# Strips of 64 bytes between the seven left operands of a linear attention block with SwiGLU

## The chip, the core and the metric

The kernel runs on one core of a Trainium2 chip. The core has TensorE (matmuls; PE in the profile, its weight loads PEld), VectorE (DVE), ScalarE (ACT), GpSimd (POOL) and SyncE (SP), a working memory of 128 partitions (SBUF), an accumulator memory of eight banks (PSUM), and DMA engines that move data to and from the main memory. The metric is the device time of one execution in microseconds (us); the median of several runs is given.

## What is computed

For x of 2048 x 1024 (float32):

```python
xn = _layernorm(x, axis=-1)
s = _A_ref(xn, A_wqkv, A_wo)          # linear attention, 32 heads of 32
g = _silu(_B_ref(xn, B_w1, B_w3, B_w2))
return x + s * g
```

`_A_ref` takes q, k and v from one product with `wqkv` (1024 x 3072), applies `phi(t) = where(t > 0, t + 1, exp(t)) + 1e-6` to q and k, forms `kv = phi(k)^T v` and the sum of `phi(k)` for each head, divides `phi(q) kv` by `phi(q)` times that sum, and multiplies with `wo` (1024 x 1024). `_B_ref` is `(silu(xn w1) * (xn w3)) w2` with 3584 hidden columns.

## The kernel before

**Products.** Every large product is cut in two along each of its three dimensions, and the eight products of blocks are replaced by seven, with sums of blocks formed beforehand and afterwards (Strassen's scheme in Winograd's form). The seven right operands are called `B11, T2, T3, T1, B21, T4, B22`, their left partners `A11, S2, S3, S1, A12, A22, S4`. Each operand is held as two parts of a shorter type (`split`, L95 and L96: ScalarE rounds to the high part, VectorE subtracts to get the low part), and each product of tiles is three matmuls (`mm3`, L103 to L105): high by high, high by low, low by high. A wide matmul has a stationary operand of 128 x 128 and a moving operand of 128 x 512.

**Stages.** The tokens are taken in two halves of 1024.

1. For the first half the rows of x are loaded, normalised and turned (transposes by TensorE, L164), which fills the seven left operands, one tile a name: `operand_tiles` makes them, each of 128 partitions x 2 parts x 4 slices x 512 columns, 16,384 bytes in a partition. For the second half they are prepared meanwhile, kept in main memory (`a_d`), and loaded into the same seven places.
2. `gemm` (L447 to L499) forms one block of 256 output columns for all tokens of a half: 7 products of 4 slices x 3 matmuls, 84 matmuls. The stationary operands are the weights' tiles of the pool `pb`; the moving operands are the seven left operands, in the order A11, S2, S3, S1, A12, A22, S4. Each half has 36 such calls: 4 for keys, 4 for queries, 28 for the gate and up projections. In places two calls run side by side, product by product.
3. Between the keys and queries of the second half and its projections, `row_products` forms xn^T phi(k) (tiles `xy`, all in `pb`, into banks `g`).
4. During the second half's projections smaller work is put between the products by `catch_up`: denominators, `key_values`, and `merge_wo` (L943 and around), whose matmuls have the stationary operand `kvm` of the pool `st` and the moving operand `wos` of `pb`.
5. Attention: its right operands (`wp`, from `attention_right`) are put into the seven places of the left operands, four tiles of 4,096 bytes to a place; they are the moving operands here. The stationary ones are `X...` tiles in `pb`.
6. The second layer of the SwiGLU (`layers`): its right operands lie in the pool `pw`, which takes over the memory of the seven places and of what follows; stationary are again `X...` tiles in `pb`.

**Order.** Instructions are recorded in the order that the program writes them out, and a scheduler of the framework orders them by a simulated timeline; `tc.issue_after` pins a few. Each engine then runs its own list in order; semaphores tie them together. Loads go out on SP's queue, most stores on GpSimd's.

**Places in memory.** Pools lie one after another in a partition, in the order in which they are opened: `const`, `pb` (8 x 4,096 bytes), `pe`, `pc`, `pa` (the seven places), `praw`, `st`; `pw` is opened after `pa`, `praw` and `st` are closed. Every tile is rounded up to 32 bytes. The constants contain a tile `gap` of 79 floats (316 bytes, 320 with rounding) that nothing reads or writes. The places that matter, in bytes from the start of a partition, and their remainders modulo 512:

| tile | before | mod 512 | after | mod 512 |
|---|---|---|---|---|
| first of `pb` (stationary operands) | 17,984 | 64 | 17,664 | 256 |
| A11 | 77,376 | 64 | 77,056 | 256 |
| S2 | 93,760 | 64 | 93,504 | 320 |
| S3 | 110,144 | 64 | 109,952 | 384 |
| S1 | 126,528 | 64 | 126,400 | 448 |
| A12 | 142,912 | 64 | 142,848 | 0 |
| A22 | 159,296 | 64 | 159,296 | 64 |
| S4 | 175,680 | 64 | 175,744 | 128 |
| first of `praw` | 192,064 | 64 | 192,256 | 256 |
| `kvm` (in `st`) | 227,968 | 128 | 228,160 | 320 |
| first of `pw` (after `pa` is closed) | 77,376 | 64 | 77,056 | 256 |

The last tile ends at 228,992 bytes before and at 229,184 after, of 229,376.

Of the kernel before, what the change touches and what calls it, by code (L numbers as in the profile page):

```python
# [9 lines left out]
F32 = mybir.dt.float32  # L10
FR = mybir.dt.float32r
# [5 lines left out]
P = 128  # L17
C = 512
# [4 lines left out]
def tile_linear_attention_times_swiglu(  # L23
# [14 lines left out]
    ND = D // P  # L38
# [8 lines left out]
    const = ctx.enter_context(tc.tile_pool(name="const", bufs=1))  # L47
# [12 lines left out]
    for i in range(P // DH):  # L60
        nc.vector.memset(hmask[i * DH:(i + 1) * DH, i * DH:(i + 1) * DH], 1.0)

    const.tile([P, 79], F32, name="gap")
    zacc = const.tile([P, ND], F32, name="zacc")
    nc.vector.memset(zacc, 0.0)

# [16 lines left out]
    AOPS = ["A11", "S2", "S3", "S1", "A12", "A22", "S4"]  # L83
# [28 lines left out]
    pa = era1.enter_context(tc.tile_pool(name="pa", bufs=1))  # L112
# [53 lines left out]
        return turned, low  # L166

    def operand_tiles(h):
        return {n: pa.tile([P, 2, ND // 2, C], FR, tag=n, name=f"{n}_{h}") for n in AOPS}

    def keep_rows(h, i, n, t):

# [474 lines left out]

    def half(h):
        A = operand_tiles(h)

        def keys(pair, **how):
# [494 lines left out]
    def hiddens(i, m):  # L1146
        return left(m, lambda n: h_d[i][m // NT][:, PLACE[n][m % NT]], (FB[i][1] - FB[i][0]) // 2, f"B{i}")
# [7 lines left out]
    def second_weights(i, n, k):  # L1155
        if (i, n, k) not in asked:
            ask(i, n, k, small)
        return asked[i, n, k]
# [110 lines left out]
    def layer_place(n, i, k):  # L1269
# [4 lines left out]
                      lambda n, _, k, i=i: second_weights(i, n, k),  # L1274
                      lambda m, i=i: hiddens(i, m), lambda m, t, n: acc[m][:, t, n],
# [32 lines left out]
```

## Time and profile before

| | |
|---|---|
| median of 3 runs | 2347.4 us (2346.8 to 2353.08) |
| the profiled execution | 2349.84 us, its span 2348.1 us |
| TensorE busy | 2300.6 us (98% of the span), 10,368 matmuls |
| VectorE, ScalarE, GpSimd busy | 76%, 39%, 29% |
| moved by DMA | 479.69 MB, 204 GB/s |

The span runs from the first to the last instruction. A busy share is an average over stages; matmuls overlap one another, so a duration (about 390 ns for a wide one) is longer than the distance from one start to the next. In a row of a timeline the first number is the start in us, the second the duration in us; in a row by line, three numbers with strokes are minimum, median and maximum of the duration in ns. A name before the arrow is what an instruction writes, those after it what it reads; buffer numbers are left out, so `A` stands for A11, A12 and A22, and `S` for S1 to S4.

### The profile page before, as it was taken

Reading aid. Unit: us, or ns where it says so; the run is one execution under the profiler, and the core shown is the slowest. Engines: PE = TensorE matmul, PEld = TensorE weight load, DVE = VectorE, ACT = ScalarE, POOL = GpSimd, SP = SyncE. Lnnn points to the kernel's source line nnn. Section 1 sums busy time; section 2 is a strip of 40 time slices with the busy share of each in tenths; the row PEclk is TensorE's granted clock in tenths of the full one; section 3 lists DMA queues with packets and bytes.
Section 4 is the critical chain, followed back from the end, with each engine's and each line's share of the span. In section 5 each row is a group of like instructions: output and inputs, shape, how many; then the busy total and the mean of one; then the engine's idle time right before and its main releaser. Section 6 shows DMA issues by size and latency. Waiting matters only on the chain.

```text
span 2348.1 us, 30976 instructions
## 1 busy us (share of the span) xinstructions
PE 2300.6 (98%) x10368; PEld 1890.5 (81%) x10368; DVE 1780.3 (76%) x2830; ACT 924.7 (39%) x1639; POOL 689.8 (29%) x854
## 2 busy tenths in 40 slices
PE   6999999999999999999999999999999999999997
PEld 5788888888887888777888888888887888888876
DVE  8887888888777775657867788887745666766798
ACT  5555343433232555433332433334324534242433
POOL 4220333376866221001423344342310000000033
PEclk9999999999999999999999999999999999999999
DMA  6555455576668646776756666665656566665688
GB/s 233 179 184 180 153 184 184 170 226 218 226 209 314 221 146 202 253 258 203 224 180 183 191 193 212 205 213 174 224 158 196 180 188 176 222 215 177 192 267 258
DMA packets 353695, 479.69 MB, mean 204 GB/s; under 512 B 24208, under 2 KB 262800, under 8 KB 353424
## 3 DMA queue, kind: packets, MB, share of 16 engines
q1 hardware_dynamic: 315808, 357.63, 48.2%
q0 software_dynamic: 37728, 120.09, 15.6%
q8 instruction: 81, 1.33, 0.2%
q14 instruction: 78, 0.64, 0.1%
HBM read 306.71 MB, written 174.59 MB: 205 GB/s over the span
## 4 chain that ended last, share of the span: by engine, by line
PE 73%; issue 5%; DVE 4%; DMA 3%; ACT 1%; POOL 0%; SPq 0%; DVEq 0%; POOLq 0%; ACTq 0%
PE g L103 2%; PE g L104 2%; PE g L105 2%; PE dB L104 1%; PE dB L105 1%; PE dB L103 1%; PE aB L103 1%; PE cB L103 1%; PE cB L104 1%; PE aB L104 1%; PE aB L105 1%; PE cB L105 1%; PE bB L105 1%; PE bB L104 1%; PE bB L103 1%
## 5 line engine op out<-in xcount | busy, mean ns | idle before, releaser
L750 POOL DMA_DIRECT2D h_d<-sg x112 | 82.8, 740 | 256.8 <-DVE sg L746 166.3
L1063 POOL DMA_DIRECT2D u_d<-uB x32 | 17.3, 541 | 407.6 <-DVE uB L1046 345.8
L96 DVE TENSOR_TENSOR xy<-xy,xy 128x512 fp32r<-128x512 f32 x112 | 72.9, 686 | 65.4 <-ACT xy L95 65.3
L95 ACT CAST xy<-xy 128x512 fp32r<-128x512 f32 x112 | 65.1, 619 | 102.0 <-PE g L105 58.4
L104 PE MATMUL g<-xy,xy 128*128 128x512 f32 x224 | 87.8, 392 | 0.3 <-DVE xy L96 0.2
L105 PE MATMUL g<-xy,xy 128*128 128x512 f32 x224 | 87.3, 390 | 0.0
L103 PE MATMUL g<-xy,xy 128*128 128x512 f32 x224 | 82.7, 398 | 0.0
L517 POOL DMA_DIRECT2D y_d<-y x48 | 34.6, 721 | 140.0 <-ACT y L537 79.9
L1046 DVE TENSOR_TENSOR acc<-cB,acc 128x512 f32<-128x512 f32 x50 | 34.4, 689 | 42.9 <-PE cB L105 42.9
L1046 DVE TENSOR_TENSOR acc<-dB,acc 128x512 f32<-128x512 f32 x56 | 38.6, 689 | 30.8 <-PE dB L105 30.6
L730 POOL TENSOR_TENSOR hs<-hs,sg 128x256 f32<-128x256 f32 x56 | 60.5, 1081 | 0.1
L732 POOL TENSOR_TENSOR hs<-sg 128x256 f32<-128x256 f32 x56 | 57.3, 1023 | 0.0
L103 PEld LDWEIGHTS g<-xy,xy 128*128 128x128 f32 x224 | 41.8, 188 | 14.2 <-issue 4.5
L888 POOL DMA_DIRECT2D qs_d<-qd x32 | 18.1, 564 | 117.5 <-DVE qd L884 80.1
L1177 POOL DMA_DIRECT2D s_d<-s x32 | 17.3, 541 | 117.4 <-DVE s L1046 69.2
L733 POOL TENSOR_TENSOR hs<-sg,hs 128x256 f32<-128x256 f32 x56 | 50.6, 903 | 1.4
L104 PEld LDWEIGHTS g<-xy,xy 128*128 128x128 f32 x224 | 42.1, 188 | 10.2 <-DVE xy L96 1.4
L729 POOL TENSOR_TENSOR hs<-sg,sg 128x256 f32<-128x256 f32 x56 | 49.7, 887 | 1.2
L765 POOL TENSOR_TENSOR w<-w 128x256 f32<-128x256 f32 x28 | 28.2, 1007 | 73.0 <-DMA w<-in_B_w 73.0
L105 PEld LDWEIGHTS g<-xy,xy 128*128 128x128 f32 x224 | 42.1, 188 | 8.8
L758 POOL DMA_DIRECT2D h_d<-hs x60 | 45.8, 765 | 3.5 <-POOL hs L733 2.4
L95 ACT CAST XS4B<-rS4B 128x384 fp32r<-128x384 f32 (+1 forms) x40 | 19.7, 493 | 60.7 <-PE cB L105 41.1
(5315 smaller groups left out, 8326.9 us busy)
## 6 DMA issues: line engine op xcount, KB each, us to landing
h_d<-hs POOLq DMA_DIRECT2D x60, 256.0 KB, 3.3
h_d<-sg POOLq DMA_DIRECT2D x56, 256.0 KB, 3.7
w<-in_B_w SPq DMA_DIRECT2D x56, 256.0 KB
wt_d<-w SPq DMA_DIRECT2D x28, 512.0 KB
xy<-x_d SPq DMA_DIRECT2D x28, 512.0 KB
xy<-y_d SPq DMA_DIRECT2D x28, 512.0 KB
h_d<-hs SPq DMA_DIRECT2D x52, 256.0 KB
y_d<-y POOLq DMA_DIRECT2D x48, 256.0 KB, 3.1
```

Source lines behind the costliest of these rows:

```text
L95: nc.scalar.copy(out=hi, in_=src)
L96: return nc.vector.tensor_sub(out=lo, in0=src, in1=hi.bitcast(F32))
L103: nc.tensor.matmul(acc, lhsT=wh, rhs=ah, start=start, stop=False, skip_group_check=True)
L104: nc.tensor.matmul(acc, lhsT=wh, rhs=al, start=False, stop=False, skip_group_check=True)
L105: return nc.tensor.matmul(acc, lhsT=wl, rhs=ah, start=False, stop=stop, skip_group_check=True)
L729: e.tensor_add(out=s1, in0=a21, in1=a22)
L730: e.tensor_sub(out=s2, in0=s1, in1=a11)
L732: e.tensor_sub(out=s3, in0=a11, in1=a21)
L733: e.tensor_sub(out=s4, in0=a12, in1=s2)
L750: nc.gpsimd.dma_start(out=h_d[i][2 * h + c][:, 2 * n:4 * n + 2, k], in_=src)
L758: queue.dma_start(out=h_d[i][2 * h + c][:, 6 + 4 * e:10 + 4 * e, k], in_=o[e].rearrange("p (e s) -> p e s", s=P))
L1046: return V.tensor_add(out=c, in0=src, in1=c)
```

## The change

The tile `gap` goes, and `operand_tiles` makes, behind each of the seven left operands, a tile that nothing uses: 16 floats (64 bytes) behind the first six, 32 floats (128 bytes) behind the last. Both halves use the same seven places and strips, and so does attention. `pb`, `pe` and `pc` begin 320 bytes lower, `praw` and `st` 192 bytes higher.

```diff
-    const.tile([P, 79], F32, name="gap")
     zacc = const.tile([P, ND], F32, name="zacc")
     nc.vector.memset(zacc, 0.0)
...
     def operand_tiles(h):
-        return {n: pa.tile([P, 2, ND // 2, C], FR, tag=n, name=f"{n}_{h}") for n in AOPS}
+        A = {}
+        for i, n in enumerate(AOPS):
+            A[n] = pa.tile([P, 2, ND // 2, C], FR, tag=n, name=f"{n}_{h}")
+            pa.tile([P, 16 if i < 6 else 32], F32, tag=f"step{i}", name=f"step{i}_{h}")
+        return A
```

## The prediction, made before the changed kernel was run

> **What bounds the kernel now.** I read the page first: shares of busy time, the clock, the chain that ended last.
>
> ```profile
> span 2348.1 us, 30976 instructions
> PE 2300.6 (98%) x10368; PEld 1890.5 (81%) x10368; DVE 1780.3 (76%) x2830; ACT 924.7 (39%) x1639; POOL 689.8 (29%) x854
> PEclk9999999999999999999999999999999999999999
> PE 73%; issue 5%; DVE 4%; DMA 3%; ACT 1%; POOL 0%; SPq 0%; DVEq 0%; POOLq 0%; ACTq 0%
> ```
>
> TensorE (PE) works through 98% of the span with its clock at 9 tenths or more in every slice, and the chain is TensorE for 73%: what lengthens a matmul lengthens the kernel, nearly one for one. The list of waits shows single events at its head (total, times, longest, in us):
>
> ```profile
> PE tA L164 <- DVE v L148: 11.4, 1, 11.4
> PE bk__735 L103 <- ACT S L95: 4.7, 1, 4.7
> PE cB L103 <- DVE acc L1046: 3.1, 1, 3.1
> ```
>
> Then the pace of the matmuls, from two stretches of the table of windows in which TensorE never stops:
>
> ```profile
> 1400.00:1600.00 200.00, 200.00 (x884) 165.79 (x883) 167.25 (x292) 62.28 (x104) 84.35 (x104) 1.00 0.66 207
> 1900.00:2200.00 300.00, 300.00 (x1325) 248.76 (x1324) 200.24 (x349) 99.59 (x189) 11.35 (x21) 1.00 0.60 185
> ```
>
> After the stretch come its length and TensorE's busy time with its matmuls. 200/884 and 300/1325 give 226.3 ns from start to start, in the gate and up products as in the second layer. The program has 9,792 of these 128x512 matmuls: 72 calls of `gemm` x 7 products x 12 = 6,048; row products 672; attention 672; second layer 2,352; `merge_wo` 48. Times 226.3 ns that is 2,216 of 2,348 us. So the question is whether addresses can move this pace. By line (min/median/max of a duration in ns, first and last start):
>
> ```profile
> L103 PE MATMUL g<-xy,xy x224: 388/390/502, 913.2 to 1079.2; 128*128 128x512 f32 x112
> L103 PE MATMUL bB<-T,XS2B x87: 387/390/398, 1805.5 to 2327.5; 128*128 128x512 f32 x87
> ```
>
> ```profile
> L103 PE MATMUL wp<-wos,kvm x16: 397/398/399, 1172.2 to 1350.7; 128*128 128x512 f32 x16
> L104 PE MATMUL wp<-wos,kvm x16: 388/394/399, 1172.6 to 1351.0; 128*128 128x512 f32 x16
> L105 PE MATMUL wp<-wos,kvm x16: 392/398/398, 1172.9 to 1351.2; 128*128 128x512 f32 x16
> ```
>
> Most medians are 390. Where `kvm` is the stationary operand they are 398, 394 and 398, in L103 without an exception. These 48 are the only wide matmuls whose two operands differ in their remainder modulo 512 bytes: every other place that a wide matmul reads lies 64 bytes past a multiple of 512, `kvm` 128 past one. (Slices of one weight tile are 512 bytes apart, and the pace is even over them; so only the part below 512 can matter.) The starts show it too, in the timeline:
>
> ```profile
> 1174.92 0.39 PE L103 MATMUL cg__9791<-A,T4g__9833 128*128 128x512 f32 x1
> 1175.14 0.39 PE L104 MATMUL cg__9791<-A,T4g__9833 128*128 128x512 f32 x1
> ...
> 1175.60 0.40 PE L103 MATMUL wp<-wos,kvm 128*128 128x512 f32 x1
> 1175.83 0.39 PE L104 MATMUL wp<-wos,kvm 128*128 128x512 f32 x1
> 1176.06 0.40 PE L105 MATMUL wp<-wos,kvm 128*128 128x512 f32 x1
> 1176.30 0.39 PE L103 MATMUL dg__9792<-S,B22g__9860 128*128 128x512 f32 x1
> ...
> 1176.99 0.39 PE L103 MATMUL dg__9792<-S,B22g__9860 128*128 128x512 f32 x1
> ```
>
> From 1175.60 to 1176.99 there are six matmuls: 1.39 us, against 6 x 226.3 = 1.36. So one disturbance costs about 30 ns, and nothing waits there. A stop has the same after-effect, with the remainders equal:
>
> ```profile
> 301.74 0.50 PE L103 MATMUL cg__2665<-A,T4g__2578 128*128 128x512 f32 x1 [1.39 <-DVE c22g__2697 L470]
> 302.07 0.39 PE L104 MATMUL cg__2665<-A,T4g__2578 128*128 128x512 f32 x1
> 302.31 0.40 PE L105 MATMUL cg__2665<-A,T4g__2578 128*128 128x512 f32 x1
> ...
> 303.23 0.39 PE L103 MATMUL cg__2665<-A,T4g__2578 128*128 128x512 f32 x1
> 304.14 0.39 PE L104 MATMUL cg__2665<-A,T4g__2578 128*128 128x512 f32 x1
> ```
>
> 302.07 to 303.23 are five starts in 1.16 us, 27 ns more than 5 x 226.3 (1.13); 303.23 to 304.14 are four in 0.91, which is the pace again. TensorE thus has a settled rhythm with the weight load of the next matmul; a disturbance throws it out, and it needs some five matmuls and 27 ns to come back.
>
> **The change, part by part.** No instruction is added, removed or moved, on any engine or queue, and no wait: the streams of the changed program are the same, only addresses differ. So no queue is passed and no wait added.
>
> *The gap dropped.* The pools before the strips and after them sink or rise together: `pb` and the later layer's places lie 256 past a multiple of 512, `praw` too, `kvm` 320. Between `pb`, `praw`, `kvm` and the second layer's places no difference changes: the row products (672), the second layer (2,352) and `merge_wo` (48) keep their pace. Cost 0. For VectorE, a sum whose target lies at a multiple of 256 bytes (the first call's `u`) stands beside one at 64 past it:
>
> ```profile
> L463 DVE TENSOR_TENSOR uk__342<-bk__735,uk__342 x1: 691/691/691, 71.0 to 71.0; 128x512 f32<-128x512 f32 x1
> L463 DVE TENSOR_TENSOR uk__365<-bk__871,uk__365 x1: 691/691/691, 85.6 to 85.6; 128x512 f32<-128x512 f32 x1
> ```
>
> 691 and 691: cost 0. If it were not, TensorE covers it: VectorE is busy for 76%. DMA targets outside the seven places move from 64 past a multiple of 256 to a multiple of it; no row shows a transfer at two alignments. DMA ends 3% of the chain, 70 us; a tenth of that either way, 7 us, would be the outermost, and I take 0, since nothing in the trace tells a sign. [...]
>
> *The strips.* The left operands now lie 0, 64, 128, 192, 256, 320 and 384 bytes (modulo 512) away from the right operands' remainder, in the order in which `gemm` uses them. Every product of 12 matmuls therefore begins with a new difference, 504 times. What that costs is between two ends. Upper: the long durations of the `kvm` rows last as long as the difference does, (8+4+8)/3 = 6.7 ns on each matmul of the six places that are off: 6,048 x 6/7 x 6.7 = 34.7 us. Lower: some difference runs faster than the settled one; the shortest durations of the rows above are 387 against 390, so 3 ns on 5,184 matmuls, -15.6 us. Between them, the rhythm settles anew after each change: 27 ns x 504 = 13.6 us. I take this one, since the stop's rows are the only ones that run long enough to show an end of the disturbance, and since after `kvm` the pace returns too.
>
> *Attention.* `attention_right` puts its right operands into the same seven places, four to a place; there the place changes every three matmuls, too few to settle (five were needed). 24 of 28 tiles lie in the six places that are off: 672 x 24/28 x 6.7 ns = 3.9 us. Upper the same; lower -3 ns each, -1.7.
>
> Sum: 13.6 + 3.9 = 17.5 us. It falls on TensorE's own chain, which nothing covers; waits of TensorE for VectorE may shrink by a little of it (the 3.1 us above at most). The profiled execution took 2349.84 us, 2.4 above the median of 2347.4; 2349.8 + 17.5 - 2.4 = 2364.9, 0.75% slower than the median.
>
> [...]
>
> **The rivals.** *Nothing happens.* The strips land as the diff says, but the 8 ns of `wp` come from something else about `kvm`, which lies at the far end of the memory, 227,968 bytes up, in another pool. For it: three matmuls at a time are all the evidence. Against it: `bB` above streams from places all over the upper half at 390. Time 2347.
>
> *It never settles.* 34.7 + 3.9 = 38.6 us, 2386. For it: in L103 and L105 of `wp` the medians stay at 398, the third no better than the first. Against it: the stop's rows settle.
>
> *Faster.* One or more of the differences 128 to 384 lets load and stream pass with less delay. Place: the products of S3 to S4. At -3 ns on 5,184 + 576 matmuls the time is 2330; it decides from the point where the mean over the seven products is below 226.3 ns. For it: durations under 390 exist. Against: they are single ones, and the only off difference in the trace is slow. [...]
>
> **How the numbers follow.** Settling after each product 0.40 (2365), never settling 0.30 (2386), nothing 0.14 (2347), faster 0.16 (2330). About 0.3%, 7 us, is what a measurement of this kernel can tell from no change. The first two are slower: 0.70; same 0.14; faster 0.16. The range must reach into both ends: 2338 leaves out most of the faster case (some 0.11), 2396 what is worse than never settling (0.07). The likeliest case's own range is 2355 to 2376: 20 to 50 ns a product.
>
> **What would show it.** Right: medians of `gemm`'s matmuls above 390 in A and S places other than A11, with `g` and the second layer still at 390; stretches like 1400:1600 with fewer than 880 matmuls, 1900:2200 unchanged. If settling holds, the first five of a product's twelve are long and the rest 390; if not, all twelve. Wrong: 884 in 1400:1600 again, or more than that; or a change in 1900:2200, where no difference moved.

## The result and the profile after

The changed kernel takes 2367.72 us (median of 4 runs, 2366.83 to 2369.38); the kernel before, in the same comparison, 2348.93 (4 runs, 2346.8 to 2353.08). The ratio is 1.008, with a 95% interval from 1.0067 to 1.0093: slower by 18.8 us. The profiled execution took 2366.89 us, 17.05 more than that of before.

First the page of the kernel after: the span, the busy times, the queue of GpSimd's stores (packets, MB, share of the 16 DMA engines' span) and the shares of the chain that ended last.

```profile
span 2365.1 us, 30976 instructions
PE 2323.7 (98%) x10368; PEld 1889.6 (80%) x10368; DVE 1783.0 (75%) x2830; ACT 926.4 (39%) x1639; POOL 687.2 (29%) x854
...
q0 software_dynamic: 37728, 120.09, 13.6%
...
PE 84%; issue 5%; DVE 4%; DMA 4%; POOL 1%; ACT 1%; SPq 0%; DVEq 0%; POOLq 0%; ACTq 0%
```

The count of instructions is the same on every engine. TensorE is busy for 23.1 us more; its weight loads and the other engines change by 3 us at most. The chain is TensorE for 84% in place of 73%. So the time sits inside the matmuls, and the two stretches of the table of windows say in which:

```profile
1400.00:1600.00 200.00, 200.00 (x867) 162.48 (x866) 164.60 (x288) 62.55 (x104) 82.97 (x101) 1.00 0.62 203
1900.00:2200.00 300.00, 300.00 (x1326) 248.48 (x1324) 206.13 (x361) 101.44 (x194) 11.52 (x22) 1.00 0.62 192
```

In the gate and up products 867 matmuls start in 200 us where it was 884 (230.7 ns each, not 226.3); in the second layer 1326 start in 300 us where it was 1325. The granted clock is 1.00 in both stretches, before and after: it is no effect of the clock. By line (min/median/max of a duration in ns), after:

```profile
L102 PE MATMUL g<-xy,xy x224: 389/389/500, 921.5 to 1086.5; 128*128 128x512 f32 x112
...
L102 PE MATMUL bB<-T,XS2B x87: 388/389/501, 1825.0 to 2344.4; 128*128 128x512 f32 x87
...
L102 PE MATMUL as<-wp,XA11s x28: 390/391/396, 1675.7 to 1794.4; 128*128 128x512 f32 x28
...
L103 PE MATMUL as<-wp,XA11s x28: 388/392/397, 1676.0 to 1794.7; 128*128 128x512 f32 x28
...
L104 PE MATMUL as<-wp,XA11s x28: 392/397/398, 1676.2 to 1794.9; 128*128 128x512 f32 x28
```

One row of attention before; the other two of `XA11s` have the same median:

```profile
L104 PE MATMUL as<-wp,XA11s x28: 389/390/390, 1659.0 to 1776.5; 128*128 128x512 f32 x28
```

Row products (`g`) and second layer (`bB`) stay at 389, where it was 390; attention (`as`), whose moving operands lie in the seven places, goes from 390 to 391, 392 and 397. (`mm3` is one line higher up now: L102 to L104.) The medians of `gemm`'s matmuls are 393 or 394 in six of the seven places, A11 among them, and 389 in A12. And one set of seven products in the timeline after (start in us, duration in us):

```profile
1503.75 0.40 PE L102 MATMUL bg__12565<-S,T2g__12544 128*128 128x512 f32 x1
...
1506.51 0.40 PE L102 MATMUL cg__12566<-S,T3g__12511 128*128 128x512 f32 x1
...
1509.31 0.39 PE L102 MATMUL dg__12567<-S,T1g__12562 128*128 128x512 f32 x1
...
1512.10 0.39 PE L102 MATMUL ag__12548<-A,B21g__12581 128*128 128x512 f32 x1
...
1513.71 0.39 PE L103 MATMUL ag__12548<-A,B21g__12581 128*128 128x512 f32 x1
...
1514.84 0.40 PE L102 MATMUL cg__12566<-A,T4g__12606 128*128 128x512 f32 x1
...
1515.78 0.39 PE L103 MATMUL cg__12566<-A,T4g__12606 128*128 128x512 f32 x1
...
1517.60 0.40 PE L102 MATMUL dg__12567<-S,B22g__12629 128*128 128x512 f32 x1
...
1520.40 0.39 PE L102 MATMUL au__12705<-A,B11u__12648 128*128 128x512 f32 x1
```

Twelve matmuls from one quoted start of a product to the next: S2 2.76 us, S3 2.80, S1 2.79, A12 2.74, A22 2.76, S4 2.80, where the settled pace gives 2.72. In this set only A12 comes back to that pace: its first seven take 1.61 us (230 ns each), its last five 1.13 us (226). A22 settles too, but at a slower pace: its first four take 0.94 us (235 ns each), the other eight 1.82 us (228). Over the whole execution the first four matmuls of S2 and of A22 take 233 ns each, the other eight 228.6 and 228.8; S3, S1 and S4 stay at 232 to 233 to the end of the product.

Over the whole execution, the mean from start to start for each place (some 850 matmuls each that the trace holds; distances above 260 ns, the stops, left out):

| place | difference mod 512, as the prediction has it | mod 256 | before, ns | after, ns |
|---|---|---|---|---|
| A11 | 0 | 0 | 226.8 | 230.2 |
| S2 | 64 | 64 | 227.2 | 230.2 |
| S3 | 128 | 128 | 227.3 | 232.7 |
| S1 | 192 | 192 | 227.2 | 233.0 |
| A12 | 256 | 0 | 227.0 | 228.7 |
| A22 | 320 | 64 | 227.4 | 230.3 |
| S4 | 384 | 128 | 227.0 | 232.6 |

(The difference is the place of the moving operand less that of the stationary one.) S2 and A22 go alike, and so do S3 and S4, which speaks for the difference modulo 256 and not 512. A12, 256 off, is the cheapest of all. A11, not off at all, is dear: it mostly follows S4 and takes some ten of its twelve matmuls to come back.

The account of TensorE, from the same starts: seven products +23.7 us (some 8,960 distances outside attention, 229.75 ns in place of 227.11; nearly all that changed lies in the seven places), attention +3.0 (672 x (231.31 - 226.81)), stops 38.9 us in place of 48.8 (what the distances above 260 ns have beyond 226.67). 23.7 + 3.0 - 9.9 = 16.8, of a span that is 17.0 longer.

### The profile page after: what moved, and what is told of

Same layout as the page of the kernel before. It is cut to its first block, busy times and chain, and to the rows that moved or that the text cites. A ratio compares the mean times of both kernels' runs of the same rounds, so it can differ in the third digit from the quotient of the medians.

```text
span 2365.1 us, 30976 instructions
## 1 busy us (share of the span) xinstructions
PE 2323.7 (98%) x10368; PEld 1889.6 (80%) x10368; DVE 1783.0 (75%) x2830; ACT 926.4 (39%) x1639; POOL 687.2 (29%) x854
## 3 DMA queue, kind: packets, MB, share of 16 engines
q0 software_dynamic: 37728, 120.09, 13.6%
## 4 chain that ended last, share of the span: by engine, by line
PE 84%; issue 5%; DVE 4%; DMA 4%; POOL 1%; ACT 1%; SPq 0%; DVEq 0%; POOLq 0%; ACTq 0%
PE g L102 2%; PE g L103 2%; PE g L104 2%; PE cB L102 1%; PE dB L104 1%; PE dB L102 1%; PE cB L104 1%; PE cB L103 1%; PE dB L103 1%; PE aB L104 1%; PE aB L103 1%; PE aB L102 1%; PE bB L104 1%; PE bB L103 1%; PE bB L102 1%
## 5 line engine op out<-in xcount | busy, mean ns | idle before, releaser
L104 PE MATMUL g<-xy,xy 128*128 128x512 f32 x224 | 87.1, 390 | 0.0
L102 PE MATMUL g<-xy,xy 128*128 128x512 f32 x224 | 82.5, 397 | 0.0
L102 PEld LDWEIGHTS g<-xy,xy 128*128 128x128 f32 x224 | 41.8, 188 | 14.0 <-issue 3.7
L104 PEld LDWEIGHTS g<-xy,xy 128*128 128x128 f32 x224 | 42.0, 188 | 8.9
```

The costliest lines, as they stand in the source:

```text
L102: nc.tensor.matmul(acc, lhsT=wh, rhs=ah, start=start, stop=False, skip_group_check=True)
L104: return nc.tensor.matmul(acc, lhsT=wl, rhs=ah, start=False, stop=stop, skip_group_check=True)
```

## The experiments

There are three theories. *Own pace*: each difference modulo 256 has a pace of its own, which holds as long as the difference does. *Settling*: every change of difference costs some 27 ns, and a constant difference costs nothing. *Place*: what counts is where an operand lies, not how two lie to one another. All edits below are against the changed kernel.

### No strips, no gap

```diff
     def operand_tiles(h):
-        A = {}
-        for i, n in enumerate(AOPS):
-            A[n] = pa.tile([P, 2, ND // 2, C], FR, tag=n, name=f"{n}_{h}")
-            pa.tile([P, 16 if i < 6 else 32], F32, tag=f"step{i}", name=f"step{i}_{h}")
-        return A
+        return {n: pa.tile([P, 2, ND // 2, C], FR, tag=n, name=f"{n}_{h}") for n in AOPS}
```

> Only the unused tile among the constants goes; there are no strips, so all operands move down by 320 bytes together and every difference between left and right operands is 0 again (kvm's stays 64). If only differences count, the pace is 226.7 ns everywhere and the time is that of before, 2347 to 2352 us. [...]

Measured: 2345.49 us (10 runs) against 2348.31 for before, ratio 0.9989 (0.9979 to 0.9998). The window of this kernel:

```profile
1400.00:1600.00 200.00, 200.00 (x884) 165.62 (x883) 167.14 (x290) 62.40 (x104) 85.47 (x105) 1.00 0.62 204
```

884 again: the slower pace is the strips' alone, and their price is 2367.72 - 2345.49 = 22.2 us (medians of two comparisons; the spans of the two profiled executions are 21.7 apart). The gap's removal by itself gives back 2.8 us, which by the interval can be 0.5 to 4.9: the pace of before, as expected if only differences count, and a time just below the range that was named for it.

### One distance for all seven places

With one unused tile ahead of the seven places and one behind, 512 bytes together, every product and every attention matmul has the same difference, and nothing changes from product to product. N was 64, 128, 192, 256, 32, 96, 160 and 224 bytes.

```diff
     def operand_tiles(h):
-        A = {}
-        for i, n in enumerate(AOPS):
-            A[n] = pa.tile([P, 2, ND // 2, C], FR, tag=n, name=f"{n}_{h}")
-            pa.tile([P, 16 if i < 6 else 32], F32, tag=f"step{i}", name=f"step{i}_{h}")
-        return A
+        pa.tile([P, N // 4], F32, tag="front", name=f"front_{h}")
+        A = {n: pa.tile([P, 2, ND // 2, C], FR, tag=n, name=f"{n}_{h}") for n in AOPS}
+        pa.tile([P, 128 - N // 4], F32, tag="back", name=f"back_{h}")
+        return A
```

64 bytes:

> One strip of 64 bytes ahead of A11 and 448 bytes behind S4: all seven places are 64 bytes away from the right operands, and the difference never changes inside gemm or attention. If each change of difference has to be settled and a constant one is free, this is as fast as before (2348 us, pace 226.7). If the difference itself sets the pace, the 12 matmuls of every product run like the later ones of S2 in the changed kernel, 226, 229 and 231 ns in turn, mean 228.9: 2.2 ns x 6,720 = 15 us on TensorE, part of it taken out of its waits: 2355 to 2363 us.

128 bytes:

> The same with all seven places 128 bytes away. Free if only changes cost: 2348 us. If the difference sets the pace, all products run like S3 and S4 of the changed kernel, about 232 ns from first to last: 5.4 ns x 6,720 = 36 us on TensorE; with waits giving back about a third, 2370 to 2385 us, slower than the changed kernel.

192 bytes:

> All seven places 192 bytes away, which is kvm's difference with the sign turned (-64 modulo 256). If the difference sets the pace: as S1 in the changed kernel, 233 ns in all seven, 6.4 ns x 6,720 = 43 us on TensorE, of which waits give back some 10: 2375 to 2392 us.

256 bytes:

> The same with all seven places 256 bytes away. If the difference counts modulo 256, this is a difference of 0 and as fast as before, 2347 to 2352 us, 226.7 ns; if it counts modulo 512, it is a state of its own with another pace.

32 bytes:

> All seven places 32 bytes away. If the pace follows the distance smoothly, between 226.7 and 229 ns: 2347 to 2356 us. If 0 is not the best of all differences, this or 224 may be under 226.7 ns and under 2344 us.

224 bytes:

> All seven places 224 bytes away, that is 32 on the other side. If the pace follows the distance smoothly, between 226.7 and 233 ns: 2350 to 2380 us; under 226.7 ns and under 2344 us if the best difference lies on this side.

96 bytes:

> All seven places 96 bytes away: 233.3 ns as at 32 and 128 if only 0 and 64 are better, 2382 us; another value between 226.7 and 233.3 if the pace steps with the distance.

160 bytes:

> All seven places 160 bytes away: 233.3 ns as at 128 and 192, 2382 us; or a state of its own, as 64 is.

Measured (the pace is the mean from start to start of the 672 matmuls of attention, all of which have the one difference; 96 and 160 were run once, so without an interval):

| distance, bytes | pace, ns | time, us | ratio to before |
|---|---|---|---|
| 0 (no strips, no gap) | 226.7 | 2345.49 | 0.9989 (0.9979 to 0.9998) |
| 32 | 233.3 | 2382.28 | 1.0142 (1.0127 to 1.0157) |
| 64 | 228.9 | 2355.37 | 1.0031 (1.0019 to 1.0043) |
| 96 | 233.3 | 2386.03 | one run |
| 128 | 233.3 | 2381.60 | 1.0141 (1.0126 to 1.0156) |
| 160 | 234.3 | 2387.73 | one run |
| 192 | 233.3 | 2381.49 | 1.0141 (1.0124 to 1.0158) |
| 224 | 233.3 | 2381.79 | 1.0140 (1.0125 to 1.0156) |
| 256 | 226.7 | 2345.93 | 0.9991 (0.9982 to 1.0001) |

The windows agree. At 64 bytes:

```profile
1400.00:1600.00 200.00, 200.00 (x876) 164.10 (x875) 167.59 (x294) 61.90 (x104) 83.69 (x102) 1.00 0.62 206
```

At 128 (859 also at 32, 96, 192 and 224):

```profile
1400.00:1600.00 200.00, 200.00 (x859) 160.91 (x858) 162.96 (x284) 60.82 (x101) 86.06 (x105) 1.00 0.61 202
```

At 160:

```profile
1400.00:1600.00 200.00, 200.00 (x856) 160.77 (x855) 162.81 (x284) 60.88 (x102) 85.13 (x103) 1.00 0.61 202
```

At 256:

```profile
1400.00:1600.00 200.00, 200.00 (x884) 165.61 (x883) 166.60 (x290) 61.99 (x104) 85.15 (x104) 1.00 0.61 204
```

200 us by 876, 859, 856 and 884 are 228.3, 232.8, 233.6 and 226.2 ns. That a constant difference costs nothing is refuted: with a difference that never changes the matmuls stay slow to the end of the run. So is a count modulo 512, since 256 costs nothing. At 64, 128 and 192 the time lies in the range that was expected if the difference sets the pace. The times that were named for 32 and 224, by a pace that follows the distance smoothly or has its best value there, did not come: 32 bytes off, to either side, already cost 6.6 ns.

These paces also tell how much of the changed kernel is a change's own cost. By them alone a set of seven products would cost 12 x (0 + 2.2 + 6.6 + 6.6 + 0 + 2.2 + 6.6) = 290 ns; the table of the seven places has 373. The 83 ns between them, some 6 us over 72 calls, are what the changes of difference cost on balance: settling is real, as the smaller part. At 128 the account of TensorE, made as above, closes: 8,962 matmuls x (231.15 - 227.17) = 35.7, attention 672 x (233.33 - 226.70) = 4.5, stops 40.2 us in place of 42.9: 37.5, and the spans (2380.9 and 2343.4) are 37.5 apart.

### `kvm` brought to the same remainder

```diff
-        A = {}
-        for i, n in enumerate(AOPS):
-            A[n] = pa.tile([P, 2, ND // 2, C], FR, tag=n, name=f"{n}_{h}")
-            pa.tile([P, 16 if i < 6 else 32], F32, tag=f"step{i}", name=f"step{i}_{h}")
-        return A
+        return {n: pa.tile([P, 2, ND // 2, C], FR, tag=n, name=f"{n}_{h}") for n in AOPS}
...
+            st.tile([P, 48], F32, tag="ahead", bufs=1, name=f"ahead{j}")
             kvm = st.tile([P, 2, P], FR, tag="kvm", bufs=1, name=f"kvm{j}")
```

The 192 unused bytes stand ahead of `kvm` in its own pool, at the same far end of the memory; the difference of `wos` to `kvm` goes from 192 to 0 modulo 256.

> The kernel without the gap, and 192 unused bytes ahead of kvm, so that it too lies at a multiple of 256 like its moving operand. If the place decides, the three rows of wp fall from 398, 394 and 398 ns to 390; if it is something else about kvm (its pool, its far end of the memory, the change of product), they stay. The time gains at most 48 x 7 ns and what follows each, 0.6 us: 2345 us.

The rows by line without strips and gap, with `kvm` where it was:

```profile
L102 PE MATMUL wp<-wos,kvm x16: 397/398/398, 1169.3 to 1347.8; 128*128 128x512 f32 x16
...
L103 PE MATMUL wp<-wos,kvm x16: 388/393/398, 1169.8 to 1348.0; 128*128 128x512 f32 x16
...
L104 PE MATMUL wp<-wos,kvm x16: 392/397/398, 1170.0 to 1348.3; 128*128 128x512 f32 x16
```

The same rows with `kvm` moved:

```profile
L102 PE MATMUL wp<-wos,kvm x16: 389/389/389, 1170.5 to 1348.5; 128*128 128x512 f32 x16
...
L103 PE MATMUL wp<-wos,kvm x16: 389/389/389, 1171.0 to 1348.7; 128*128 128x512 f32 x16
...
L104 PE MATMUL wp<-wos,kvm x16: 389/389/389, 1171.2 to 1348.9; 128*128 128x512 f32 x16
```

So it is neither the pool of `kvm`, nor its place at the far end, nor the change of product. Moving `kvm` changes its own remainder along with the difference, though; the next experiment tells these two apart. This kernel takes 2344.12 us (10 runs) against 2349.16, ratio 0.9981 (0.9971 to 0.999). It is the fastest of those measured here, and faster than both kernels; but 48 x 6.7 ns are 0.3 us, so nearly all of its 5 us must come from the gap's removal and the scatter between runs.

### A gap of 64 bytes, no strips

This brings every place outside the first constants back to 64 bytes past a multiple of 256, as in the kernel before, with all differences at 0.

```diff
+    const.tile([P, 16], F32, name="gap")
     zacc = const.tile([P, ND], F32, name="zacc")
...
-        A = {}
-        for i, n in enumerate(AOPS):
-            A[n] = pa.tile([P, 2, ND // 2, C], FR, tag=n, name=f"{n}_{h}")
-            pa.tile([P, 16 if i < 6 else 32], F32, tag=f"step{i}", name=f"step{i}_{h}")
-        return A
+        return {n: pa.tile([P, 2, ND // 2, C], FR, tag=n, name=f"{n}_{h}") for n in AOPS}
```

> The kernel without strips and with an unused tile of 64 bytes instead of 320 among the constants: differences all 0, but every tile behind it lies 64 past a multiple of 256 again, as before. If the small gain of the kernels without the gap comes from tiles at multiples of 256, the share of the software queue returns from 13.8% to 15.6% and the time to that of before, 2348 us. If it comes from the 320 bytes being gone, or is chance, share or time stay at 13.8% or 2345 us.

Measured: 2347.32 us (11 runs) against 2348.33, ratio 0.9998 (0.9989 to 1.0007): the time of before. Its window:

```profile
1400.00:1600.00 200.00, 200.00 (x884) 165.68 (x883) 167.23 (x292) 61.96 (x104) 84.40 (x103) 1.00 0.65 206
```

884, and 226.7 ns in attention. Here the seven places have the very addresses that they have with one distance of 64 bytes (A11 at 77,120, and so on), where the window has 876 and the pace is 228.9 ns. Among the operands of these matmuls only the stationary ones lie elsewhere, 64 bytes higher; and in the kernel without strips and gap the stationary ones lie where that slower kernel has them, with a pace of 226.7. So it is not the place of either operand that counts but the difference: *place* falls.

The queue of stores with the gap of 64 bytes:

```profile
q0 software_dynamic: 37728, 120.09, 15.7%
```

One row of its list of TensorE's waits, a wait that before had too:

```profile
PE cg__2665 L103 <- DVE c22g__2697 L470: 1.4, 1, 1.4
```

The queue without gap and strips:

```profile
q0 software_dynamic: 37728, 120.09, 13.8%
```

Same packets, same bytes, 15.7% against 13.8%; before had this:

```profile
q0 software_dynamic: 37728, 120.09, 15.6%
```

In the profiles of the eleven kernels without the old offset the share is 13.4 to 13.8%. By the list of TensorE's waits, its sum is 37.6 us before and 37.3 with the gap of 64 bytes, 32.0 to 33.0 in the three kernels with every product at the settled pace and no such gap, 29.6 to 33.1 in those with slow products. So the waits that went, went with the offset of all these places, whatever the pace; through which transfer each of them ended sooner was not followed up, and that it was a transfer at all is not shown. In the queue itself only the packets of 4,096 bytes changed: 192 ns each on average before and with the gap of 64 bytes, 167 without gap and strips. Those of 2,048 bytes took 190 to 197 in all three. In medians the offset is worth some 2 to 3 us; the interval of the gap of 64 (0.9989 to 1.0007) and that of none (0.9979 to 0.9998) overlap, so the size isn't settled better than that.

## Why the prediction was right

*The verdict and the time.* Slower was forecast, 2364.9 us and 2355 to 2376 for the likeliest case; 2367.72 came. The direction was reasoned, from the `kvm` rows; that the time is so near is in good part luck. Two terms were off and nearly cancel, and the larger one, the strips, was worked out from a mechanism that carries only the smaller part of what was measured. Against the profiled execution of before, the sum was 17.5 us and the measured difference 17.05, as +23.7 +3.0 -9.9 in place of +13.6 +3.9 and little else.

*The pace is what bounds, and addresses can move it.* This was right. The kernel's difference lies in the matmuls, with 16.8 of 17.0 us accounted for by their starts. The reading of the 48 `kvm` rows as a matter of remainders was right too, and held when `kvm` alone was moved.

*The strips: "the rhythm settles anew after each change: 27 ns x 504 = 13.6 us."* This term was mis-sized, 13.6 us for 23.7, because the step took the disturbance to be the change, after which one pace returns. The runs show that each difference has a pace of its own, and the change comes on top. The stop's rows from which the 27 ns came were taken at difference 0, and at 0 the pace does return. That it returns after `kvm` proves no settling either, since the difference is 0 again there. A12 alone, 0 modulo 256, behaves as the step says: 12 x (228.75 - 226.67) = 25 ns a product. S2 and A22 cost 42 and 44 ns: some 26 by the pace of 64 bytes (12 x 2.2) and the rest in their first four matmuls. S3, S1 and S4 cost 72, 76 and 72, a little less than their pace alone (12 x 6.6 = 79). A11 costs 42, after S4's disturbance. Together that is 373 ns for seven products, 26.8 us for 72 calls; less the 2.7 us that the products before had above 226.67 ns already, this is about the 23.7.

*"Their remainder modulo 512 bytes."* This was wrong: it is 256. The trace of before could not tell, since its one difference, 64 bytes below the settled one (`kvm`), is off by either count. By 256 two of the seven places are at 0, not one.

*Attention, 3.9 us.* It was 3.0. The price of 6.7 ns was right for most constant differences (233.3 - 226.7 = 6.6); the tiles in places with 64 or 0 modulo 256 pay less.

*The gap dropped, cost 0.* It was -2.8 us on medians. The step named the transfers and their lack of a row, and took 0 "since nothing in the trace tells a sign". The queue's share fell with the 2.8 us, from 15.6 to 13.8%: its 4,096-byte packets took 13% less (192 to 167 ns), and those of 2,048 bytes stayed at 190 to 197 ns. How that reaches the end of the kernel is not shown; what is seen is the waits that are gone with it, such as the 1.4 us of `cg__2665`.

*Waits shrink by 3.1 at most.* 9.9 us of stops went, of which 5.9 (48.8 to 42.9) are gone without the strips too; what is left for the slower pace is 4.0. The bound for the slower pace was low by little; what was missed is the gap's part.

*The rivals.* "Nothing happens" is out by the 22.2 us of the strips. "It never settles" was nearer in kind than the case that was chosen, since it lets the cost last as long as the difference. It came near the pace of three of the seven places (6.0 to 6.3 ns against its 6.7) and would have been right, to 5 us, for one constant distance of 128: 2381.60 against its 2386. In the changed kernel it fails at A11, A12, S2 and A22. "Faster" is out for every multiple of 32 bytes: no distance gave less than 226.7 ns.

*What would show it.* 867 (fewer than 880) and 1326 (unchanged) were as named. Five long matmuls and then 390 were not seen, save roughly at A12, where it took seven; and A11, which was to stay at 390, went to 393.

Some things are left open. Which access meets which was not tried apart: that the rhythm is one with the weight load of the next matmul was the prediction's estimate, and the runs show only that the difference between the two operands counts (226.7 ns at 0, 228.9 at 64 with the same moving operands). Why 64 costs 2.2 ns and 192, the same distance the other way, 6.6 is not explained by any run; nor is the extra nanosecond at 160. Distances that aren't multiples of 32 bytes were not tried.

## What to carry to other kernels

Where long rows of matmuls run back to back, put the stationary and the moving operands at the same remainder modulo 256 bytes: 226.7 ns from start to start here, against 228.9 to 234.3 at the other multiples of 32 bytes. A few rows can give it away, medians of 395 to 398 beside 389 for the same shape; but in the kernel with all seven places 128 bytes away one of the three lines of `kvm`, itself 192 bytes off, has 388, so the number of matmuls that start in a stretch without stops (884 in 200 us here, against 856 to 876) is the surer sign. A duration that looks like noise on the 48 matmuls of `kvm` (192 bytes off) is worth 36 us when 6,720 have it. And when a term of the sum is taken from a recovery after a stop, ask whether the disturbance in question goes away at all. Here it lasts as long as its cause: 859 matmuls in 200 us at a constant 128 bytes.

## What the runs showed of the hardware

- A 128x512 matmul with its weight load starts every 226.7 ns when the two operands differ by 0 or 256 bytes modulo 512, every 228.9 at 64, every 233.3 at 32, 96, 128, 192 and 224, every 234.3 at 160 (mean over 672 matmuls of attention; 96 and 160 from one run each). These hold for as long as the distance does: 876, 859, 856 or 884 matmuls in 200 us of the gate and up products, with the granted clock at 1.00.
- The distance, moving less stationary, has a sign: +64 gives 228.9 ns, -64 (192) gives 233.3. It is the difference that counts: with the moving operands at the same addresses, stationary operands 64 bytes higher bring 228.9 to 226.7.
- A change of difference costs something of its own. At 0 the 226.7 ns come back in some 7 matmuls (A12) or 10 (A11); at 64 the first four matmuls take 233 ns, the others 228.6 to 228.8.
- 37,728 packets of stores take 15.6 to 15.7% of the DMA engines' time in the two kernels whose tiles lie 64 bytes past multiples of 256, and 13.4 to 13.8% in the eleven without that offset. The 4,096-byte packets among them take 192 ns on average with the offset and 167 without, the 2,048-byte packets the same.
